# Attention on one Trainium2 core: the stationary exponentials of the second product in two halves of 64 queries

## The chip, the cores and the metric

The kernel runs on one core of a Trainium2 chip. The metric is the time of one execution in device microseconds; the median of three runs is what the change will be measured by. One more execution was recorded by the hardware profiler, and every row below comes from it.

## The reference

Only the first of three stages is touched, attention over 4 batches of 8 heads, 576 tokens and 64 dimensions a head:

```python
q_rot, k_rot = rotate(q), rotate(k)
scores = scale * np.matmul(q_rot, k_rot.transpose(0, 1, 3, 2))
scores = scores - np.max(scores, axis=-1, keepdims=True)
attn = np.exp(scores)
attn = attn / (np.sum(attn, axis=-1, keepdims=True) + 1e-09)
out = np.matmul(attn, v)
```

Its output goes as x (2304 tokens of 512) through a soft mixture of experts (32 slots, 8 experts, 512 to 1024 to 512) and then through a gated layer (512 to 2048 to 512). All inputs and outputs are float32.

## The kernel before, in words

The 32 (batch, head) units are worked on as 16 pairs of heads, `p` = 0 to 15. A pair is opened (`open_pair`) and then goes through four steps (`step(p, idx)`, idx 1 to 4). The queries of a pair are split in two stretches `h`: 256 queries (two blocks of 128) and 320 (three blocks of 128, the last two overlapping by half, `TOK`). The keys are split in four chunks `c` of 128 for each head and a fifth, `c == 4`, which holds the remaining 64 keys of both heads.

A step issues on TensorE, in this order: the first product for the row maxima of a coming pair (`max_diff`, L301, tile `psmx`), the scores of two key chunks (`scores`, L344, tile `st`, 16 matmuls in which the two heads use the two row halves of the array), the second product for the maxima (`max_second`, L315), in one step of each pair the transpose of the maxima (`max_rows`, L325, tile `psm`, a 64-column stationary operand), and last the product of exponentials and values for the stretch before the current one (`pv`, tile `u`): chunks 0 and 1 in the stretch's first step, chunks 2, 3 and 4 in its second. For chunks 0 to 3 a block of 128 keys by 128 queries of exponentials (`et`) is the stationary operand and the values of a head with a column of ones (`vt`, 65 columns) are the moving one, L374. Chunk 4 serves both heads at once with 130 moving columns, L370. Each of these float32 calls stands in the trace as two pairs of a weight load and a matmul. `evict` then divides by the row sum on VectorE (L384 to L386).

ScalarE takes the exponentials (L347), the relu of the first maximum product (L307) and some roundings; VectorE reduces the maxima (L318) and adds up the rotary terms (L263, L269); GpSimd multiplies q and k by the rotary tables (L257, L260); SyncE issues the loads. What runs between the products is placed by hand: `tasks` maps a step number `g` to functions, so that a load for pair `p` is issued at 10p - 30, its rotary work from 10p - 26 on. The kernel has a manual schedule; each engine works in the order of the program. The scores have two buffers in PSUM, `psmx` and `u` one each. After attention the expert weights stream in (L825, L846), and the last stage, over 200 us, is the gated layer (L1003 to L1123); one of its small products, L1043 (tile `g_ps`), uses four 32-column tiles of the array, one for each quarter of the output partitions.

Of the kernel before, what the change touches and what calls it, by code (L numbers as in the profile page):

```python
# [60 lines left out]
def attn_softmoe_mlp_kernel(ctx: ExitStack, tc: tile.TileContext, qk, v, cst, phi, w1, w2, w_in, w_out, out):  # L61
    nc = tc.nc
    pe, act, dve, pool, sp = nc.tensor, nc.scalar, nc.vector, nc.gpsimd, nc.sync
# [116 lines left out]
    with tc.manual_schedule():  # L180
        with ExitStack() as t1:
# [32 lines left out]
            raw, vt = {}, {}  # L214
# [117 lines left out]
            et, er, u_ps, xt, xq = {}, {}, {}, {}, {}  # L332
# [29 lines left out]
            def pv(p, h, c, t=None):  # L362
                if (p, h) not in u_ps:
                    u_ps[p, h] = ps_u.tile([128, 512], F32, tag="u", name=f"u{p}_{h}") if t is None else t
                    u_ps[p, h, "n"] = 0
                u, n = u_ps[p, h][:, 0:390].rearrange("p (t h d) -> p t h d", t=3, h=2), u_ps[p, h, "n"]
                for i, o in enumerate(TOK[h]):
                    if c == 4:
                        e = er[p].rearrange("p h s -> p (h s)")[:, QO[h] + o:QO[h] + o + 128]
                        pe.matmul(u[:, i].rearrange("p h d -> p (h d)"), lhsT=e, rhs=vt[p][:, c].rearrange("p h d -> p (h d)"),  # L370
                                  start=n == 0 and i == 0, stop=n == 4, skip_group_check=True)
                    else:
                        for hd in range(2):
                            pe.matmul(u[:, i, hd], lhsT=et[p, h, c][:, hd, o:o + 128], rhs=vt[p][:, c, hd],  # L374
                                      start=n == 0 and i + hd == 0, stop=n == 4, skip_group_check=True)
                u_ps[p, h, "n"] = n + 1

            def evict(p, h):
# [277 lines left out]
            def step(p, idx):  # L656
                n, c0 = 2 * p + idx // 3, 2 * ((idx - 1) % 2)
                h = n % 2
                us = plan.get((p, idx), ())
                for u in us:  # L660
                    max_diff(*u)
                for i in range(2):
                    scores(p, h, c0 + i)
                a = divmod(n - 1, 2)
                for u in us:
                    max_second(*u[0:2])
                run(10 * p + 2 * idx)
                if n and n < 2 * NPAIR - 1:
                    if c0 == 0:
                        r = rows.get((p, idx))  # L670
                        if r:
                            max_rows(r)
                        pv(*a, 0)
                        pv(*a, 1)
                    else:
                        for c in (2, 3, 4):
                            pv(*a, c)
                if n and n < 2 * NPAIR - 1 and c0:
                    evict(*a)
                run(10 * p + 2 * idx + 1)  # L680
# [420 lines left out]
    for n, (j, k) in enumerate(seq):  # L1101
        ghi, glo = gt.pop((j, k))
        for i in range(NI):
# [12 lines left out]
            if k == 15:  # L1116
                o = g2.tile([128, DM], F32, tag="os", bufs=6, name=f"os{j}_{i}")
# [52 lines left out]
```

## Time and profile before

| | us |
|---|---|
| median of 3 runs | 654.64 |
| lowest and highest run | 652.83, 657.73 |
| the profiled execution | 660.41 |
| span of its trace | 658.6 |
| TensorE busy | 625.9 |
| VectorE, ScalarE, GpSimd busy | 318.3, 310.9, 115.0 |

The span runs from the first to the last instruction. Attention lies between about 34 and 373 us, the expert weights between 373 and 426, the gated layer after that. A matmul's busy time includes the time it takes to pass through the array, so durations of matmuls that follow one another overlap, and the pace of a group is read from the starts.

### The profile page before, as it was taken

The numbers are of one execution on the slowest core, as the hardware profiler recorded it, in microseconds if no ns is written. First come the engines' busy times: TensorE is split into PE (matmuls) and PEld (weight loads), VectorE is DVE, ScalarE is ACT, GpSimd is POOL, SyncE is SP. The second block draws the span as 40 slices with busy tenths as digits, with TensorE's granted clock in tenths as the row PEclk, the third lists the DMA queues.
The fourth block names the chain that finished last, engine by engine and source line by source line (L and its number), as shares of the span: only waits on it lengthen the run. The fifth ranks groups of instructions, "written<-read, shape, count | busy, mean of one in ns | idle before, by whom it ended". The sixth has DMA issues, their size and how long they took to land. (4 is left out here: it accounts for less than half of the span.)

```text
span 658.6 us, 12152 instructions
## 1 busy us (share of the span) xinstructions
PE 625.9 (95%) x4758; PEld 513.9 (78%) x4758; DVE 318.3 (48%) x826; ACT 310.9 (47%) x627; POOL 115.0 (17%) x97
## 2 busy tenths in 40 slices
PE   5789999999999999999999999988999999999997
PEld 2479888988898889888889733466878888888886
DVE  4761456344634553465322214377865544454442
ACT  3452555465545654555443213279774433453442
POOL 3752213330333303330000001121320000000000
PEclk9695999999999999999999979999999999999999
DMA  7250654454445433455326688963400200020002
GB/s 263 78 190 25 222 180 138 159 171 156 127 150 179 127 122 112 147 191 162 128 59 253 241 306 309 400 231 129 128 1 0 97 0 1 1 96 1 0 1 96
DMA packets 36761, 88.51 MB, mean 134 GB/s; under 512 B 10560, under 2 KB 11872, under 8 KB 34784
## 3 DMA queue, kind: packets, MB, share of 16 engines
q1 hardware_dynamic: 36694, 87.73, 39.1%
q8 instruction: 37, 0.61, 0.4%
q14 instruction: 20, 0.16, 0.1%
q10 hardware_dynamic: 10, 0.00, 0.0%
HBM read 78.20 MB, written 7.60 MB: 130 GB/s over the span
## 5 line engine op out<-in xcount | busy, mean ns | idle before, releaser
L374 PEld LDWEIGHTS u<-v,e 128*128 128x128 f32 x1280 | 152.8, 197 | 11.0 <-issue 5.1
L374 PE MATMUL u<-v,e 128*128 128x65 f32 x1280 | 160.9, 282 | 0.0
L318 DVE CUSTOM_DVE_ANT_0 relu<-psmx,relu 128x288 f32<-128x288 f32 x138 | 58.0, 454 | 121.8 <-ACT e L347 106.9
L1010 DVE TENSOR_TENSOR hps<-hps,g 128x384 f32<-128x384 f32 x96 | 49.8, 561 | 84.3 <-ACT g L1007 84.0
L347 ACT ACTIVATE e<-st 128x512 f32<-128x512 f32 (+1 forms) x128 | 76.6, 652 | 18.4 <-PE st L344 18.2
L1108 PE MATMUL ops<-wo_hi,ghi 128*128 128x512 f32 x216 | 84.6, 392 | 0.0
L1109 PE MATMUL ops<-wo_lo,ghi 128*128 128x512 f32 x216 | 84.4, 391 | 0.0
L1110 PE MATMUL ops<-wo_hi,glo 128*128 128x512 f32 x216 | 84.3, 390 | 0.0
L307 ACT ACTIVATE relu<-psmx 128x576 f32<-128x576 f32 x61 | 39.5, 649 | 94.1 <-issue 51.8
L1007 ACT ACTIVATE g<-hps 128x384 f32<-128x384 f32 x96 | 42.3, 490 | 82.2 <-PE hps L1003 81.9
L260 POOL TENSOR_TENSOR raw<-raw,tab 128x576 f32<-128x576 f32 x30 | 44.7, 1492 | 191.4 <-DMA raw<-in_qk_dram 176.2
L1016 DVE TENSOR_TENSOR glo<-hps,ghi 128x384 fp32r<-128x384 f32 x96 | 49.4, 552 | 4.9 <-ACT ghi L1013 1.8
L1013 ACT ACTIVATE ghi<-hps 128x384 fp32r<-128x384 f32 x96 | 45.6, 493 | 10.1 <-DVE hps L1010 10.1
L1110 PEld LDWEIGHTS ops<-wo_hi,glo 128*128 128x128 f32 x216 | 40.5, 188 | 8.4
L1109 PEld LDWEIGHTS ops<-wo_lo,ghi 128*128 128x128 f32 x216 | 40.6, 188 | 7.5 <-issue 0.4
L1108 PEld LDWEIGHTS ops<-wo_hi,ghi 128*128 128x128 f32 x216 | 40.5, 188 | 7.5 <-issue 0.2
L257 POOL TENSOR_TENSOR raw<-raw,tab 128x576 f32<-128x576 f32 x29 | 43.5, 1499 | 0.0
L344 PE MATMUL st<-hi 64*128 64x256 f32 (+1 forms) x256 | 41.3, 316 | 0.1
L344 PE MATMUL st<-hi,lo 64*128 64x256 f32 (+1 forms) x256 | 38.9, 297 | 0.0
L344 PE MATMUL st<-lo,hi 64*128 64x256 f32 (+1 forms) x256 | 38.9, 297 | 0.0
L344 PE MATMUL st<-mq,neg_a 64*128 64x256 f32 (+1 forms) x256 | 38.8, 296 | 0.0
L384 DVE TENSOR_SCALAR r<-u 128x4 f32<-128x4 f32 (+1 forms) x32 | 5.2, 163 | 66.8 <-PE u L370 59.1
(210 smaller groups left out, 968.0 us busy)
## 6 DMA issues: line engine op xcount, KB each, us to landing
w<-in_w_dram SPq DMA_DIRECT2D x64, 512.0 KB
raw<-in_qk_dram SPq DMA_DIRECT2D x14, 1152.0 KB
w_out_raw<-in_w_out_dram SPq DMA_DIRECT2D x16, 512.0 KB
w_in_raw<-in_w_in_dram SPq DMA_DIRECT2D x12, 512.0 KB
v<-in_v_dram SPq DMA_DIRECT2D x16, 325.0 KB
out_dram<-os SPq DMA_DIRECT2D x18, 256.0 KB
raw<-in_qk_dram SPq DMA_DIRECT2D x4, 576.0 KB
w_in<-w_in SPq DMA_DIRECT2D x8, 256.0 KB
```

The source lines that it names most:

```text
L257: eng.tensor_tensor(out=r[:, i, 0, w], in0=r[:, i, 0, w], in1=tab[:, 0, w], op=ALU.mult)
L260: eng.tensor_tensor(out=r[:, i, 1, w], in0=r[:, i, 1, w], in1=tab[:, 1, w], op=ALU.mult)
L318: dve.tensor_tensor_reduce(out=r[:, hd], in0=t[hd], in1=r[:, hd], scale=1.0, scalar=-3.0e38, op0=ALU.add, op1=ALU.max, accum_out=mxs[p % 2 ...
L344: pe.matmul(st[:, hd, 0:n], lhsT=a, rhs=b, start=i == 0, stop=i == 3, skip_group_check=True)
L347: act.activation(out=e[:, :, 0:n], in_=st[:, :, 0:n], func=ACTF.Exp, scale=0.125)
L374: pe.matmul(u[:, i, hd], lhsT=et[p, h, c][:, hd, o:o + 128], rhs=vt[p][:, c, hd], start=n == 0 and i + hd == 0, stop=n == 4, skip_group_ch ...
L1010: dve.tensor_tensor(out=t[i], in0=t[i], in1=g[i], op=ALU.mult)
L1013: act.activation(out=ghi[:, i], in_=t[i], func=ACTF.Copy)
L1016: dve.tensor_tensor(out=glo[:, i], in0=t[i], in1=ghi[:, i].bitcast(F32), op=ALU.subtract)
L1108: pe.matmul(t, lhsT=a, rhs=wo_hi[k], start=k == 0, stop=False)
L1109: pe.matmul(t, lhsT=a, rhs=wo_lo[k], start=False, stop=False)
L1110: pe.matmul(t, lhsT=b, rhs=wo_hi[k], start=False, stop=k == 15)
```

## The change

For chunks 0 to 3 each 128-query block of stationary exponentials is given to the array as two blocks of 64 queries. The first writes output partitions 0 to 63, the second 64 to 127, of the same PSUM tile. The moving operand is the same for both. Chunk 4 stays as it is, with 128 columns.

```diff
                     else:
                         for hd in range(2):
-                            pe.matmul(u[:, i, hd], lhsT=et[p, h, c][:, hd, o:o + 128], rhs=vt[p][:, c, hd],
-                                      start=n == 0 and i + hd == 0, stop=n == 4, skip_group_check=True)
+                            for q in (0, 64):
+                                pe.matmul(u[q:q + 64, i, hd], lhsT=et[p, h, c][:, hd, o + q:o + q + 64], rhs=vt[p][:, c, hd],
+                                          start=n == 0 and i + hd == 0, stop=n == 4, skip_group_check=True)
```

## Rows read from the trace of the kernel before

**Rows 1.** The page: span, and the granted TensorE clock in 40 slices, tenths.

```profile
span 658.6 us, 12152 instructions
PEclk9695999999999999999999979999999999999999
```

**Rows 2.** Stretches: length, busy time of each engine (count), granted clock, DMA share, GB/s.

```profile
46.00:63.00 17.00, 16.26 (x86) 15.41 (x88) 4.61 (x13) 5.15 (x10) 5.69 (x4) 0.52 0.19 69
63.00:373.00 310.00, 304.69 (x2939) 272.61 (x2938) 138.91 (x437) 153.58 (x281) 62.26 (x44) 1.00 0.47 154
373.00:426.00 53.00, 49.67 (x401) 19.85 (x400) 18.04 (x53) 12.57 (x29) 2.05 (x3) 0.94 0.93 340
```

**Rows 3.** The page's costliest groups: line, shapes, count, busy us, mean ns.

```profile
L374 PE MATMUL u<-v,e 128*128 128x65 f32 x1280 | 160.9, 282 | 0.0
```

**Rows 4.** Timeline of TensorE from 206 us: start, length, merged instructions.

```profile
205.84 2.89 PE L374 MATMUL u<-v,e 128*128 128x65 f32 x24
208.57 0.89 PE L370 MATMUL u<-v,er 128*128 128x130 f32 x6
209.38 0.40 PE L301 MATMUL psmx<-kd,hi 64*128 64x288 f32 x2
...
211.00 0.43 PE L325 MATMUL psm<-cst_sb,mx 128*64 128x128 f32 x2
211.37 2.00 PE L374 MATMUL u<-v,e 128*128 128x65 f32 x16
```

**Rows 5.** Weight loads of single lines: duration min/median/max ns, first and last start.

```profile
L374 PEld LDWEIGHTS u<-v,e x1280: 186/192/333, 35.9 to 373.1; 128*128 128x128 f32 x183
...
L325 PEld LDWEIGHTS psm<-cst_sb,mx x32: 132/136/231, 18.8 to 341.7; 128*64 128x64 f32 x32
...
L1043 PEld LDWEIGHTS g_ps<-w_in_n,so x64: 106/110/110, 430.0 to 452.2; 128*32 128x32 f32 x64
```

**Rows 6.** Timeline of TensorE and its weight loads, four 32-column tiles in turn.

```profile
430.01 0.87 PE L1043 MATMUL g_ps<-w_in_n,so 128*32 128x96 f32 x32
...
430.01 0.65 PEld L1043 LDWEIGHTS g_ps<-w_in_n,so 128*32 128x32 f32 x32 [0.25 <-issue]
...
440.30 1.08 PE L1043 MATMUL g_ps<-w_in,so 128*32 128x128 f32 x32
```

**Rows 7.** Timeline of TensorE from 200 us: a change of the array's shape.

```profile
201.15 0.40 PE L315 MATMUL psmx<-hi 64*128 64x288 f32 x2 [0.37 <-ACT relu L307]
201.48 2.89 PE L374 MATMUL u<-v,e 128*128 128x65 f32 x24
```

**Rows 8.** Timeline of TensorE from 43 us, where the granted clock is low.

```profile
46.74 0.61 PE L315 MATMUL psmx<-hi 64*128 64x288 f32 x2 [1.69 <-ACT relu L307]
...
55.07 5.38 PE L374 MATMUL u<-v,e 128*128 128x65 f32 x24
60.25 1.61 PE L370 MATMUL u<-v,er 128*128 128x130 f32 x6
```

**Rows 9.** Waits from 100 to 340 us: total us, times, longest.

```profile
PE psmx L315 <- ACT relu L307: 3.7, 10, 0.4
```

**Rows 10.** Timelines of ScalarE and VectorE beside Rows 4.

```profile
206.30 0.69 ACT L135 ACTIVATE hw<-w_in_raw 128x512 f32<-128x512 f32 x1
209.87 0.65 ACT L307 ACTIVATE relu<-psmx 128x576 f32<-128x576 f32 x1 [2.88 <-issue]
...
206.44 0.45 DVE L318 CUSTOM_DVE_ANT_0 relu<-psmx,relu 128x288 f32<-128x288 f32 x1
...
209.49 0.17 DVE L384 TENSOR_SCALAR r<-u 128x6 f32<-128x6 f32 x1 [2.59 <-PE u L370]
```

**Rows 11.** Timelines of SyncE's queue, GpSimd and VectorE: one pair's load and rotary work.

```profile
92.55 0.33 SPq L223 DMA_DIRECT2D raw<-in_qk_dram  x1
...
97.90 1.43 POOL L260 TENSOR_TENSOR raw<-raw,tab 128x576 f32<-128x576 f32 x1 [14.72 <-DMA raw<-in_qk_dram]
...
112.71 0.75 DVE L263 TENSOR_TENSOR raw<-raw 128x576 f32<-128x576 f32 x1
```

## Prediction

> **What bounds the kernel now.** I read the page first: the span is 658.6 us and the granted clock is at its high level nearly throughout [rows 1]. The table of stretches then says which engine sets the pace of attention. From 63 to 373 us TensorE is busy 304.7 of 310 us, while VectorE has 138.9 and ScalarE 153.6, so they have half their time to spare [rows 2]. After 373 us the DMA share is 0.93, and that stage lives on the expert weights, not on attention. The costliest group of the page is L374, the line that the change touches: 1280 load and matmul pairs [rows 3]. Waits of TensorE in attention are few: the longest group is 3.7 us in 240 us [rows 9]. So attention ends when TensorE has worked off its list, and what L374 loses there is gained until another engine ends later.
>
> The timeline gives the pace of L374. Twenty-four pairs start at 205.84 and the next group at 208.57: 2.73 us, 114 ns a pair [rows 4]. Which half of a pair sets that pace? The group behind it moves 130 columns in place of 65 and needs (0.89 - 0.275) / 5 = 123 ns, with the first start to the last, and 0.275 us as the length of one matmul at this place. Twice the moving columns cost 9 ns, so the pace is not the moving stream. It is the weight load: loads last 110 ns for 32 columns, 136 for 64 and 192 for 128 [rows 5], thus 0.81 to 0.88 ns a column on top of a fixed latency, and 128 columns occupy 104 to 112 ns. L374 loads 128 columns of float32 for every 65 that it moves.
>
> **What the change does to that.** 640 calls (16 pairs of heads, 5 query blocks, 4 chunks, 2 heads) are 1280 pairs now and become 2560, each with 64 stationary columns. One half needs, on its own half of the array, 52 to 56 ns for the load by the slope above. The full pair's 114 ns exceed its 104 to 112 ns by 2 to 10 ns; with the same addition a half's load takes 58 to 62 ns. The moving stream of a half I take from the four-tile product: 32 pairs with 96 columns start within 0.87 - 0.25 = 0.62 us, 20 ns apart, and with 128 columns within 1.08 - 0.27 = 0.81 us, 26 ns apart [rows 6]. Four tiles share that, so one pair holds its tile for 80 and 104 ns, 0.82 ns a column, and 65 columns hold it for 53 ns. Load and stream of a half are nearly equal, and the load is the longer.
>
> Everything hangs on whether the two halves of the array do this at the same time. Rows 6 speak for it twice. The streams of four tiles overlap, for one alone would need 80 ns and they start every 20. The loads overlap too: 32 loads of 32 columns start within 0.65 - 0.11 = 0.54 us, 17 ns each, where 32 columns one after another would need 26 to 28 ns by the slope. So I take two halves at once: 60 / 2 = 30 ns a pair, between 27 (the stream alone, 53 / 2) and 35 (the burst's 17.4 ns for 32 columns, as if loads went no faster than that, twice). No row shows 64-column tiles in turn; 30 lies nearest to the 26 ns of the 128-column burst, whose tiles are loaded and streamed in the same proportion.
>
> The sum: of the 1280 pairs 48 ran at the low clock, the blocks at 47 and 55 us, with (60.25 - 55.07) / 24 = 216 ns a pair [rows 8]. Now 1232 x 114 + 48 x 216 = 140.4 + 10.4 = 150.8 us. After, 2464 x 30 + 96 x 56 = 73.9 + 5.4 = 79.3 us. Gain 71.5 us.
>
> **What is added.** Chunk 4 keeps its 128-column shape and follows 64-column blocks, so that the array changes shape once more in each of 32 stretches. The price of such a change: the two loads of L325, also 64 columns, start at 211.00 and 211.11 and the 128-column L374 at 211.37, 0.26 us after the second where 0.11 would be its own pace, hence 0.15 us [rows 4]. The bounds are 0 and the whole 0.33 us between L315 and L374 [rows 7]; I take 0.15, both sides being float32 like here: 32 x 0.15 = 4.8 us. In 15 steps L325 itself stands before L374, and there the change of shape falls away: 15 x 0.15 = 2.2 us back. Net loss 2.6 us (0 to 10).
>
> The sequencer hands out 2560 pairs in place of 1280. It starts pairs 20 ns apart in a burst of 32 [rows 6], and blocks will have 32 or 48. [...]
>
> **What is late next.** The blocks of L374 shrink from 2.7 to 1.4 us (24 pairs) and from 1.8 to 0.95 (16). In the cover of such a block ScalarE finishes its exponentials and one rounding, and VectorE two maxima. Beside rows 4 ScalarE was done at 206.99 and then idle for 2.88 us; VectorE was done with the maxima at 206.9 and idle for 2.59 [rows 10]. The block and its chunk-4 tail would now end near 208.1 in place of 209.38, after both. In the step that opens a pair the wait of 0.37 us for the relu [rows 7, 9] stays. The loads: a pair's q and k are asked for at 92.55, GpSimd starts at 97.90, its second multiplication ends 2.8 us later, near 100.7, and VectorE adds at 112.71 [rows 11]; 12 us of slack against a pair that becomes some 4 us shorter. What I deduct: 1.8 us at the start, where the two blocks before 46 us run into the wait of 1.69 us for relu [rows 8]; 0.3 us in each of 14 pairs for waits too small to see, 4 us; 2 us at the end, where attention hands over to a stage at a DMA share of 0.93 [rows 2]. Together 8 us (0 to 16).
>
> 71.5 - 2.6 - 8 = 60.9 us off the profiled execution's 660.4: 599.5. The median stands at 654.64 / 660.41 = 0.991 of that execution, so 594 us.
>
> **The rivals.** One: loads and streams overlap only in part, halfway between 30 and 60 ns, because the two halves share one supply of weights. 2464 x 45 + 96 x 84 = 118.9 us, a gain of 31.9, less 2.6 and 4 for waits: 635, or 630 as a median. For it: rows 6 show 32-column tiles, whose four loads overlap by no more than 1.6. Against it: their starts leave no gap.
>
> Two, the other side: pairs go one after another, be it that one weight path serves both halves or that the sequencer doesn't get them out faster. Each then costs 58 to 62 ns, and the block has twice as many: 2464 x 60 + 96 x 112 = 158.6, 7.8 us more than now, with the changes of shape 10.4 us: 670.8, or 665 as a median. It decides at 56 ns a pair: above that the change loses. For it: L374 is paced by its loads, and the number of loaded columns doesn't fall. Against it: the 17 ns of rows 6.
>
> Three: loads don't run beside matmuls of the same rows at all, 58 + 53 = 111 ns a pair, 2560 x 111 = 284 us, 133 more than now: near 790. [...] The trace disagrees: a full pair would need 104 + 53 = 157 ns by that, and 114 were measured [rows 4].
>
> Four: the change does nothing, the halves being handled like the whole: 655.
>
> **How the numbers follow.** Forecast 0.76, rival one 0.09, two 0.11, three 0.01, four 0.03. About 1% is what a measurement of this kernel can tell from no change. Forecast and rival one are faster by more than that, 0.85. Rival two has 0.07 on the slow side and 0.04 within 1% (58 ns would give 660), rival four is within: faster 0.85, same 0.07, slower 0.08. The range: 27 ns a pair and no waits add 7.7 and 8 us, 579; rival one ends it at 630. Within the forecast, 35 ns and twice the waits give 615.
>
> **What would show it.** Right: L374 with 2560 pairs, 48 of them within some 1.45 us at the high clock, attention's end near 312 us in place of 373, the stage after it as long as before. A pace of 58 or more in the block is rival two. If the pace is near 30 and the time above 615, look for new waits of L315 on relu, of L301 on the maxima, or for stretches at the low clock: at 46.74 us a wait of 1.69 us came before 16 us at half clock with TensorE busy [rows 2, 8], and a second such place would cost 8 us. The forecast is wrong in its base if 64-column tiles don't overlap as 32-column ones do.

## The result, and the profile after

The changed kernel takes 590.73 us as a median of four executions (586.46 to 593.13), against 654.7 us before: a ratio of 0.901, 95% interval 0.895 to 0.907. The forecast was 594, its range 579 to 630. The profiled execution took 593.13 us with a span of 591.4, so 67.2 us less than the span of before [rows 1]; the medians lie 64.0 us apart.

First the page of the changed kernel: the span, and the groups of the changed line (L375 there, the weight load beside it). Columns as in [rows 3].

```profile
span 591.4 us, 14712 instructions
...
L375 PE MATMUL u<-v,e 128*64 128x65 f32 x2560 | 92.1, 225 | 1.6 <-PE psm L325 1.6
L375 PEld LDWEIGHTS u<-v,e 128*64 128x64 f32 x2560 | 83.4, 139 | 11.3 <-issue 3.7
```

Twice the pairs, and 92.1 us busy in place of 160.9 [rows 3]. The stretches of the changed kernel answer to [rows 2], with attention ending near 307.5 us in place of 373:

```profile
46.00:63.00 17.00, 14.98 (x246) 13.54 (x245) 8.39 (x30) 9.80 (x18) 5.54 (x4) 0.90 0.47 166
63.00:307.00 244.00, 237.04 (x4016) 204.60 (x4016) 136.36 (x425) 149.50 (x273) 62.95 (x44) 1.00 0.57 189
...
307.50:360.00 52.50, 48.84 (x417) 19.81 (x417) 18.27 (x53) 13.22 (x30) 2.71 (x3) 0.93 0.97 359
360.00:591.40 231.40, 222.94 (x1128) 182.87 (x1116) 128.12 (x252) 119.94 (x272) 17.91 (x13) 1.00 0.16 59
```

The two stages behind attention are as long as they were (52.5 and 231.4 us against 53.0 and 658.6 - 426.0 = 232.6). What attention gained reached the end. TensorE still has the fullest row in attention, 237.0 of 244 us; VectorE and ScalarE came up to 56% and 61%, so neither took over. The timeline of TensorE answers to [rows 4]:

```profile
173.29 1.62 PE L375 MATMUL u<-v,e 128*64 128x65 f32 x48
174.84 0.94 PE L370 MATMUL u<-v,er 128*128 128x130 f32 x6
175.70 0.40 PE L301 MATMUL psmx<-kd,hi 64*128 64x288 f32 x2
...
177.34 0.32 PE L325 MATMUL psm<-cst_sb,mx 128*64 128x128 f32 x1
177.35 0.33 PE L375 MATMUL u<-v,e 128*64 128x65 f32 x2
177.50 0.27 PE L325 MATMUL psm<-cst_sb,mx 128*64 128x128 f32 x1
177.61 1.10 PE L375 MATMUL u<-v,e 128*64 128x65 f32 x30
```

Forty-eight pairs start within 1.62 - 0.22 = 1.40 us, 29.7 ns apart (0.22 us is the median length of one). Taken singly, the starts in this block come in twos, 6 or 7 ns apart, and such a couple follows every 59 ns: two halves run at a time. The last starts near 174.69 and the 128-column L370 at 174.84. Where L325 stands before L375, as here, there is no gap left: both have 64 columns, and their pairs even interleave.

### The profile page after: what moved, and what is told of

The parts are those of the page before. It is cut to its first block, busy times and chain, and to the rows that moved or that the text cites. A ratio compares the mean times of both kernels' runs of the same rounds, so it can differ in the third digit from the quotient of the medians.

```text
span 591.4 us, 14712 instructions
## 1 busy us (share of the span) xinstructions
PE 557.5 (94%) x6038; PEld 444.7 (75%) x6038; DVE 318.3 (54%) x826; ACT 311.6 (53%) x627; POOL 114.7 (19%) x97
## 5 line engine op out<-in xcount | busy, mean ns | idle before, releaser
L375 PE MATMUL u<-v,e 128*64 128x65 f32 x2560 | 92.1, 225 | 1.6 <-PE psm L325 1.6
L375 PEld LDWEIGHTS u<-v,e 128*64 128x64 f32 x2560 | 83.4, 139 | 11.3 <-issue 3.7
L307 ACT ACTIVATE relu<-psmx 128x576 f32<-128x576 f32 x61 | 39.5, 650 | 48.7 <-issue 22.3
L344 PE MATMUL st<-hi 64*128 64x256 f32 (+1 forms) x256 | 41.3, 315 | 0.1
L344 PE MATMUL st<-hi,lo 64*128 64x256 f32 (+1 forms) x256 | 39.1, 298 | 0.0
L344 PE MATMUL st<-lo,hi 64*128 64x256 f32 (+1 forms) x256 | 39.0, 297 | 0.0
L344 PE MATMUL st<-mq,neg_a 64*128 64x256 f32 (+1 forms) x256 | 39.0, 297 | 0.0
L1004 PE MATMUL hps<-cs,gs 128*128 128x384 f32 x96 | 26.6, 345 | 3.6 <-DVE glo L1017 1.9
```

The lines of the kernel that those rows point to most:

```text
L344: pe.matmul(st[:, hd, 0:n], lhsT=a, rhs=b, start=i == 0, stop=i == 3, skip_group_check=True)
L375: pe.matmul(u[q:q + 64, i, hd], lhsT=et[p, h, c][:, hd, o + q:o + q + 64], rhs=vt[p][:, c, hd], start=n == 0 and i + hd == 0, stop=n == 4, ...
```

## Experiments

Theory A is the prediction's: the weight load sets the pace, and two column halves load and stream at the same time. Theory B: a 64-column pair simply takes 30 ns, wherever it stands. Each kernel is the changed one with the edit shown; only the first is shown against the kernel before. Times are medians, and each ratio is to executions of the kernel before in the same series, with its 95% interval.

**The order of the halves.**

```diff
+                for q in (0, 64) if c < 4 else ():
+                    for i, o in enumerate(TOK[h]):
+                        for hd in range(2):
+                            pe.matmul(u[q:q + 64, i, hd], lhsT=et[p, h, c][:, hd, o + q:o + q + 64], rhs=vt[p][:, c, hd],
+                                      start=n == 0 and i + hd == 0, stop=n == 4, skip_group_check=True)
                 for i, o in enumerate(TOK[h]):
                     if c == 4:
...
-                    else:
-                        for hd in range(2):
-                            pe.matmul(u[:, i, hd], lhsT=et[p, h, c][:, hd, o:o + 128], rhs=vt[p][:, c, hd],
-                                      start=n == 0 and i + hd == 0, stop=n == 4, skip_group_check=True)
```

> The same 2560 pairs of 64 stationary columns, but in each chunk all blocks and heads of queries 0 to 63 first, then all of 64 to 127: runs of 8 or 12 pairs on one half of the array. Theory A (the gain is that the two halves load and stream at the same time): within a run nothing overlaps, 58 to 62 ns a pair, blocks of 48 pairs near 2.9 us and a time near 655 to 665 us; if the array looks ahead across a run's border, somewhat less. Theory B (64-column loads are simply handed out at 30 ns a pair): the order is indifferent, 30 ns a pair and 590 us.

Measured: 629.23 us (ratio to before 0.961, 0.955 to 0.968). Timeline of TensorE of this kernel (L370 is the changed line here, L375 is chunk 4):

```profile
169.26 2.48 PE L370 MATMUL u<-v,e 128*64 128x65 f32 x48
171.67 0.94 PE L375 MATMUL u<-v,er 128*128 128x130 f32 x6
...
174.44 1.50 PE L370 MATMUL u<-v,e 128*64 128x65 f32 x32
175.87 0.40 PE L301 MATMUL psmx<-kd,hi 64*128 64x288 f32 x2
```

Runs of 12 pairs on a half: (2.48 - 0.22) / 47 = 48 ns. Runs of 8: (1.50 - 0.22) / 31 = 41 ns. Theory B falls: the same instructions in another order cost up to 18 ns more each. Theory A's 655 to 665 us was not reached either; some overlap at each border remains.

**All on one half.** To have the price without any border, the pairs of chunks 1 to 3 were all put on the first half:

```diff
-                                pe.matmul(u[q:q + 64, i, hd], lhsT=et[p, h, c][:, hd, o + q:o + q + 64], rhs=vt[p][:, c, hd],
+                                r = q if n in (0, 4) else 0
+                                pe.matmul(u[r:r + 64, i, hd], lhsT=et[p, h, c][:, hd, o + q:o + q + 64], rhs=vt[p][:, c, hd],
```

> Chunks 1 to 3 put both blocks of 64 queries on output partitions 0 to 63, so on the same half of the array; queries 64 to 127 then lack these chunks and queries 0 to 63 hold both sums. Pairs, columns and their order are those of the changed kernel, only the place differs. Theory A (halves at the same time): 1920 pairs go one after another, 58 to 62 ns, and 1920 x 30 ns more than the changed kernel, 645 to 655 us. Theory B (a 64-column pair simply needs 30 ns): 590 us. By-half order left 41 ns in runs of 8 and 48 ns in runs of 12; a block without any border should show the whole price.

Measured: 644.12 us (ratio 0.983, 0.978 to 0.988). Timeline of TensorE, a block of chunks 2 and 3:

```profile
175.09 3.01 PE L376 MATMUL u<-v,e 128*64 128x65 f32 x48
178.03 0.94 PE L370 MATMUL u<-v,er 128*128 128x130 f32 x6
```

(3.01 - 0.22) / 47 = 59.3 ns, exactly twice the 29.7 ns of alternating halves. That is the price of rival two, inside its 58 to 62 ns. With the other 640 pairs at 59.3 as well the kernel would take 644.1 + 640 x 0.0296 = 663 us by this estimate, where rival two gave 665. The mechanism of the gain is thus shown: not the smaller load, but two of them at a time.

**Runs of four.**

```diff
-                        for hd in range(2):
-                            for q in (0, 64):
+                        for q in (0, 64):
+                            for hd in range(2):
```

> Both heads of queries 0 to 63, then both of 64 to 127: runs of 4 pairs on a half in place of 2. If the array starts matmuls strictly in order, a run of n pairs costs 59 x (1 - 1/n) ns a pair: 44 ns, near 627 us. If it looks ahead across a border by the 2.3 pairs that runs of 8 and 12 suggest (41 = 59 x (1 - 2.4/8), 48 = 59 x (1 - 2.2/12)): still 30 ns and 590 us.

Measured: 595.4 us, from two executions (ratio 0.909, 0.902 to 0.916). Timeline of TensorE:

```profile
174.31 1.67 PE L375 MATMUL u<-v,e 128*64 128x65 f32 x48
175.91 0.94 PE L370 MATMUL u<-v,er 128*128 128x130 f32 x6
```

(1.67 - 0.22) / 47 = 30.9 ns. The 44 ns of a strict order are refuted; four in a row on a half cost 1.2 ns a pair.

**What sets the pace of a half.**

```diff
+                        d0 = 32 if 0 < n < 4 else 0
...
-                                pe.matmul(u[q:q + 64, i, hd], lhsT=et[p, h, c][:, hd, o + q:o + q + 64], rhs=vt[p][:, c, hd],
+                                pe.matmul(u[q:q + 64, i, hd, d0:], lhsT=et[p, h, c][:, hd, o + q:o + q + 64], rhs=vt[p][:, c, hd, d0:],
```

> Chunks 1 to 3 leave out the first 32 value columns of each head (33 moving columns in place of 65), so those outputs hold chunk 0 and 4 alone. If the load of a half sets its pace: 29 to 30 ns a pair as with 65 columns, within 2 us of the changed kernel. If the stream sets it: 33 columns hold a half for 27 ns, the pace falls to what the load or the sequencer allows, 20 to 28 ns, 4 to 19 us less.

Measured: 588.56 us (ratio 0.898, 0.892 to 0.904). Timeline of TensorE, chunks 2 and 3:

```profile
167.99 1.59 PE L376 MATMUL u<-v,e 128*64 128x33 f32 x48
169.51 0.94 PE L370 MATMUL u<-v,er 128*128 128x130 f32 x6
```

(1.59 - 0.22) / 47 = 29.1 ns with half the moving columns. The stream is not what a half waits for. That leaves the load or the sequencer, which the next kernel tells apart.

**Four quarters.**

```diff
-                            for q in (0, 64):
-                                pe.matmul(u[q:q + 64, i, hd], lhsT=et[p, h, c][:, hd, o + q:o + q + 64], rhs=vt[p][:, c, hd],
+                            for q in (0, 32, 64, 96):
+                                pe.matmul(u[q:q + 32, i, hd], lhsT=et[p, h, c][:, hd, o + q:o + q + 32], rhs=vt[p][:, c, hd],
```

> Four quarters of 32 queries in place of two halves, 5120 pairs. Theory A: each quarter's stream of 53 ns is the longer part, four overlap, 13 ns a pair, 106 ns for a call in place of 119: near 582 us. If the sequencer's floor is the 20 ns that the trace of before shows in a burst: 160 ns a call, 640 x 41 ns more, near 617 us. Theory B (the 30 ns are what the sequencer needs for a pair): 240 ns a call, near 668 us.

Measured: 603.92 us (ratio 0.921, 0.914 to 0.928). Timeline of TensorE: a block with a wait in its middle, and one without; then the page's group of the line, and last the queue q8 in the list of DMA queues (packets, MB, share), first of this kernel and then of the changed one.

```profile
168.52 0.47 PE L375 MATMUL u<-v,e 128*32 128x65 f32 x17
170.11 0.89 PE L375 MATMUL u<-v,e 128*32 128x65 f32 x47 [1.12 <-issue]
...
175.99 1.58 PE L375 MATMUL u<-v,e 128*32 128x65 f32 x96
177.51 0.41 PE L301 MATMUL psmx<-kd,hi 64*128 64x288 f32 x2
```

```profile
L375 PE MATMUL u<-v,e 128*32 128x65 f32 x5120 | 90.9, 222 | 9.1 <-issue 8.3 <-PE psm L325 0.5
```

```profile
q8 instruction: 67, 1.10, 0.8%
...
q8 instruction: 47, 0.77, 0.5%
```

An undisturbed block has 96 pairs within 1.58 - 0.22 = 1.36 us, 14.3 ns a pair. So the sequencer is not what holds a half at 29.7 ns; of load, stream and sequencer only the load is left. One rival is untested: that a pair holds its tile for some 58 ns at least, whatever it loads. Halves hold theirs for 2 x 29.1 = 58 ns (33 columns) and 59 (65), and quarters, which load half as much, for 4 x 14.3 = 57, where the prediction's 0.82 ns a column gives 53 for the stream. That full blocks, with twice the columns, take 114 ns speaks for the load. But pairs of L439 (transposes, 128 stationary columns on 32 rows, 32 moving ones) start every 62 ns in the changed kernel's trace, so the columns alone don't fix the time of a load. Quarters with 33 moving columns would decide it.

A call of eight pairs costs 114 ns against 119 with halves, little better. The kernel is nevertheless 13 us slower than with halves. Its trace shows 8.3 us in which TensorE stood before this line and waited for nothing that the view names ("issue"), as 1.12 us at 170.11 and 1.35 at 74.09. In the changed kernel the matmuls of the line have 1.6 us of idle time before them, all of it put down to L325. The queue q8, which the page calls "instruction", moved 1.10 MB here, where the program has 2 x 8598 matmuls and weight loads, 0.77 MB in the changed kernel with 2 x 6038, and 0.61 MB in the kernel before with 2 x 4758: 64 bytes for each of them, three times over. That the supply of instructions ran short in the quarters is no more than the author's reading of these numbers: no view shows what the waits end with, and no run varied the supply.

**Chunk 4 in halves as well.**

```diff
-                        pe.matmul(u[:, i].rearrange("p h d -> p (h d)"), lhsT=e, rhs=vt[p][:, c].rearrange("p h d -> p (h d)"),
-                                  start=n == 0 and i == 0, stop=n == 4, skip_group_check=True)
+                        for q in (0, 64):
+                            pe.matmul(u[q:q + 64, i].rearrange("p h d -> p (h d)"), lhsT=e[:, q:q + 64], rhs=vt[p][:, c].rearrange("p h d -> p (h d)"),
+                                      start=n == 0 and i == 0, stop=n == 4, skip_group_check=True)
```

> Chunk 4 in halves as well, so that no 128-column shape follows the 64-column one. Theory A with the price of a change of shape as predicted: 32 x 0.15 us fall away, and 160 pairs of 123 ns become 320 of 53 ns (130 columns at 0.82 ns, two at a time), 2.6 us: 7 us less, 583 to 584 us. If the change of shape costs nothing: 2.6 us less, 588 us.

Measured: 590.5 us (ratio 0.902, 0.897 to 0.907). It was run again later beside another kernel:

> Chunk 4 in halves with the conversions where they were: 588 to 592 us, as in its first runs.

Measured: 588.76 us (0.902, 0.900 to 0.904). Timeline of TensorE in the first of these, a stretch of three query blocks and one of two:

```profile
169.88 1.62 PE L376 MATMUL u<-v,e 128*64 128x65 f32 x48
171.33 0.84 PE L371 MATMUL u<-v,er 128*64 128x130 f32 x12
172.09 0.40 PE L301 MATMUL psmx<-kd,hi 64*128 64x288 f32 x2
...
176.66 1.15 PE L376 MATMUL u<-v,e 128*64 128x65 f32 x32
177.64 0.61 PE L371 MATMUL u<-v,er 128*64 128x130 f32 x8
178.18 0.40 PE L301 MATMUL psmx<-kd,bd 128*128 128x288 f32 x1
```

From block to L301 the first stretch takes 2.21 us in place of 2.41 in the changed kernel's timeline. The second takes 1.52, where the changed kernel's trace has 1.55 (180.26 to 181.81): behind it the next matmul has the full 128*128 shape, which the unsplit chunk 4 shared, and the change of shape that left its front came back at its end. The first start of L301 comes 0.20 us after the last of L371, and 0.03 us after the last of L370 in the changed kernel, there in 14 stretches. Expected were 7 us in all; a gain of at most some 3 us is left, which the intervals don't tell from none.

**A wait that the shorter blocks uncovered.** In the changed kernel TensorE waited twice by 0.8 us ahead of L375, at 90.63 and at 145.13. Timelines of TensorE and VectorE at the first:

```profile
89.38 0.43 PE L325 MATMUL psm<-cst_sb,mx 128*64 128x128 f32 x2
90.63 1.15 PE L375 MATMUL u<-v,e 128*64 128x65 f32 x32 [0.81 <-PE psm L325]
...
86.32 1.48 DVE L138 TENSOR_SCALAR wf_early<-hwo 128x512 uint32<-128x512 uint32 x1
87.83 1.80 DVE L141 SCALAR_TENSOR_TENSOR wf_early<-w_out_raw,wf_early 128x512 uint32<-128x512 uint32 x1
89.56 0.15 DVE L385 TENSOR_SCALAR r<-u 128x6 f32<-128x6 f32 x1
89.75 0.19 DVE L386 RECIPROCAL r<-r 128x6 f32<-128x6 f32 x1
89.97 0.56 DVE L387 TENSOR_TENSOR x<-u,r 128x384 f32<-128x384 f32 x1
```

The view names L325, which had ended 0.8 us earlier. L375 writes `u` anew and needs the division that reads the old one; that ended at 90.53, held up behind two conversions. Two kernels moved the conversions, both on top of chunk 4 in halves:

```diff
-                at(g + 6, lambda k=k: cv["o", k][1](), lambda k=k: cv["o", k][2]())
+                at(g + 7, lambda k=k: cv["o", k][1](), lambda k=k: cv["o", k][2]())
```

> Chunk 4 in halves too, and the two VectorE steps of the four early w_out conversions one task step later, behind the division by the row sums. In the changed kernel L375 waited about 0.8 us for that division at up to four places, where the conversions in front of it took 1.48 and 1.80 us beside GpSimd. If these waits are real losses: 2 to 3 us, with chunk 4 another 3 to 4, together 584 to 586 us. If later work absorbs them: no different from the changed kernel.

> The changed kernel itself, beside the next one on the same chip: 587 to 593 us.

Measured: 593.64 us with the move (ratio 0.907, 0.903 to 0.911), 590.9 for the changed kernel in the same series (0.904, 0.899 to 0.908). The second of the two texts is for that repeat of the changed kernel. Timelines of the moved version, VectorE and then TensorE:

```profile
86.27 1.43 DVE L138 TENSOR_SCALAR wf_early<-hwo 128x512 uint32<-128x512 uint32 x1
87.74 1.77 DVE L141 SCALAR_TENSOR_TENSOR wf_early<-w_out_raw,wf_early 128x512 uint32<-128x512 uint32 x1
...
90.32 0.40 PE L301 MATMUL psmx<-kd,hi 64*128 64x288 f32 x2 [2.06 <-DVE mx L318]
...
92.17 2.00 PE L376 MATMUL u<-v,e 128*64 128x65 f32 x32
```

The conversions now stand ahead of the maxima, and L301 waits 2.06 us for those; the block behind it takes 2.00 us where 1.15 is usual, and the granted clock over 60 to 100 us was 0.96, against 1.00 for chunk 4 in halves without the move. Nothing was gained. In the other kernel `g + 7` is `g + 10`:

> Chunk 4 in halves, and the VectorE steps of the four early conversions in the pair's last step (task step g + 10), where GpSimd has ended its rotary work. Theory: the conversions then take 0.42 and 0.69 us, no wait of L376 for the division and none of L301 for the maxima remains: 2 to 4 us under the kernel with the conversions at g + 7, 587 to 590 us. Rival: they only move the wait again, 592 us or more.

Measured: 588.78 us (ratio 0.902, 0.899 to 0.904), against 588.76 for chunk 4 in halves without the move, in the same series. The conversions are short now, 0.42 and 0.69 us in the groups of this kernel, and the wait is gone, yet the time is the same. Part of the wait came up elsewhere, as the rival said: between 60 and 300 us L315 waits 5.9 us in all for the relu, with single waits of up to 0.75, where chunk 4 in halves without the move has 4.4 and none above 0.4. The theory on the wait held, the gain expected from it didn't come.

```profile
L141 DVE SCALAR_TENSOR_TENSOR wf_early<-w_out_raw,wf_early 128x512 uint32<-128x512 uint32 x4 | 2.8, 692 | 0.1
L138 DVE TENSOR_SCALAR wf_early<-hwo 128x512 uint32<-128x512 uint32 x4 | 1.7, 420 | 0.0
```

No version clearly beats the changed kernel.

## Why the prediction was right, step by step

- **The load sets the pace of L374**: for the halves this is shown by exclusion, with the 33-column and the quarter kernels, and the least time of a pair on its tile is left as a rival. For the full blocks of before it rests on [rows 4, 5], as predicted.
- **Two halves at a time, 30 ns a pair**: 29.7 measured, and 59.3 without overlap, where 60 stood. The prediction's first argument for it was circular: that a stream of four tiles takes 80 ns alone had been worked out from the 20 ns between starts by taking four at a time. That two halves overlap rested on the loads of [rows 6] until the kernels with other orders showed it.
- **The sum**: forecast 79.3 us for L374 after. Measured 2560 x 29.7 = 76.0, plus 1.05 for one block of 48 pairs that took 2.67 us near 48 us, partly at the low clock; 77.0. The gain on the line is 150.8 - 77.0 = 73.8 us, not 71.5. The forecast had left 48 pairs' worth of blocks at half clock, as in [rows 8]; they ran almost wholly at the high one; no run shows what decided that.
- **What is given back**: forecast 2.6 + 8 = 10.6 us. It can't be read from the two spans, because the granted clock differed between the two executions (next point). Where both ran at the high clock throughout, from the first score matmul (L344) of the ninth step to that of the sixty-first, it can: 276.6 us before (from 73.0 us), 226.0 after (from 64.1), so 50.6 us in 13 pairs of heads, 3.9 us a pair. The paces alone would give 13 x (80 x 0.114 - 160 x 0.0297) = 56.8. Given back are 6.2 us in 13 pairs, where the forecast's 2.6 and 4 us make 5.4 for as many. The terms: the change of shape before chunk 4 is 174.84 - 174.69 - 0.03 = 0.12 us against the 0.15 taken, 3.1 us in 26 stretches; L370 itself took 1.3 us longer; two waits of 0.8 us are 1.6; and L325 gave 1.9 back. The other 2.1 are small: blocks of 32 pairs at 30.1 ns, and a dearer step from L375 to the next matmul.
- **The start, and luck**: the 1.8 us taken for the start were not tested. The wait for the relu that stood at 46.74 [rows 8] stands at 48.14 now, although the two blocks before it had gained 1.3 us. But the first block of L375 already starts at 38.22 where L374 started at 35.94. No changed instruction runs before it; the granted clock does differ, low (0.5) from 28.3 to 38.5 us here and only up to 29.5 before. In turn it is low from 46.5 to 63.6 us before, and only from 48.7 to 52.2 here. Over the whole span the low level took 39 us before and 27 after. So part of the 67.2 us between the two spans is the clock's; 16 pairs of heads at 3.9 make 62 us by the estimate from the steady stretch. That the forecast of 594 came within 4 us rests on 30 ns and on the terms per pair of heads; the last few us are luck.

The first two lines are the kernel before, the others the changed one; the third number from the end is the granted clock:

```profile
20.00:40.00 20.00, 16.46 (x125) 12.86 (x125) 12.87 (x30) 11.60 (x23) 11.55 (x8) 0.76 0.35 104
40.00:60.00 20.00, 18.31 (x115) 17.02 (x115) 9.22 (x22) 6.43 (x12) 10.51 (x7) 0.66 0.35 119
...
20.00:40.00 20.00, 16.40 (x122) 12.65 (x123) 13.75 (x30) 10.58 (x21) 11.45 (x8) 0.62 0.34 104
40.00:60.00 20.00, 17.98 (x284) 16.01 (x282) 10.12 (x29) 11.24 (x21) 11.09 (x8) 0.91 0.40 137
```

- **Cover**: ScalarE and VectorE kept up, as argued from [rows 10]; the one exception, the division behind two slow conversions, was not seen. The loads kept up, and the stage behind attention moved forward whole; no loss at its start can be seen.
- **The rivals**: one (half overlap) and four fall with 29.7 ns. Two falls for alternating halves, yet its price is right for halves that do not alternate. Its other cause, a sequencer that gets the pairs out no faster, does not bind here: 96 pairs came 14.3 ns apart. Three falls too: it would need 111 ns a pair, and even on a single half the trace has 59.3. In the changed kernel loads run beside matmuls that use the same 128 rows: the 48 loads of the block at 173.29 take 1.48 us from 173.28 on, its 48 matmuls 1.62.

## What to carry to other kernels

Where a stationary operand is loaded for few moving columns, read the pace of the pairs from the starts, and compare it with the load and with the stream. Here a pair with 128 stationary columns took 114 ns; split onto two column tiles, a pair with 64 took 29.7 where successive calls alternated between the tiles and 59.3 where they stayed on one. The gain is in the alternation, not in the smaller load: of 64 us the same halves in other orders gave back 4.7 and 38.5, and on a single half, for three chunks of four, 53. Count the instructions too: quarters were little faster in a block (114 ns a call against 119) and lost 13 us as a kernel, with 8.3 us of idle time before their line. When blocks shrink, look for the work on other engines that the long blocks had covered: here it was two waits of 0.8 us.

## What the runs showed of the hardware that was not expected

- Runs of pairs on the two halves overlap at their borders. With runs of n pairs on a half the pace was 29.7 (n = 2), 30.9 (4), 41 (8) and 48 ns (12), and 59.3 without borders. In the by-half kernel a block has four runs and so three borders. An estimate from these paces: if three pairs overlap at each border, 3 x 3 of 47 steps saved leave 59.3 x (47 - 9) / 47 = 48 ns in runs of 12, as measured, and 59.3 x (31 - 9) / 31 = 42 in runs of 8, where 41 was measured. A strict order of starts would overlap one, and the 2.3 of the expectation for runs of four came from counting four borders a block.
- Quarters reached 14.3 ns a pair in a block and lost 13 us as a kernel. TensorE stood for 8.3 us before their matmuls and waited for nothing that the view names; q8 moved 64 bytes for each matmul and weight load, here as in the kernels before and after the change.
- VectorE's conversions took up to 1.5 and 1.8 us, or 0.42 and 0.69, in the same kernel. In attention each of those over 1 us (six, 1.17 to 1.80) ran beside GpSimd's rotary multiplications, after it each (three, 1.20 to 1.64) beside other work of GpSimd; those with nothing on GpSimd beside them took 0.43 and 0.69 at most.
